# Spectral mixing with the complex filter product finished on VectorE and GpSimd, a return transform in 32-row tiles, and one fp32 copy of the filter

## The chip, the cores and the metric

The kernel runs on one core of one Trainium2 chip. A core has a matrix engine (TensorE, "PE" in the profile; its weight loads are listed apart as "PEld"), a vector engine (VectorE, "DVE"), an activation engine (ScalarE, "ACT"), a general engine (GpSimd, "POOL") and a queue engine that only starts transfers (SyncE, "SP"). Each works through its own instruction list in order. The metric is device microseconds (us) of one execution; lower is better.

## What is computed

```python
def _attn_ref(x, filt_r, filt_i):          # x: (8, 3072, 256), filters: (1537, 256)
    X = np.fft.rfft(x, axis=1)
    F = (filt_r + 1j * filt_i)[None, :, :]
    Y = X * F
    y = np.fft.irfft(Y, n=x.shape[1], axis=1)
    return y.astype(np.float32)

def _moe_ref(x, w1, w2, w_out):            # x: the result above as (24576, 256)
    h1 = x @ w1                            # w1, w2: (256, 1024)
    h2 = x @ w2
    g = np.maximum(h1, h2)
    return (g @ w_out).astype(np.float32)  # w_out: (1024, 256)
```

So each of the 8 batches is filtered along its 3072 positions (a real Fourier transform, a complex product with a filter, the transform back), and every position then goes through a maxout layer.

## The kernel before

**The transform** is split as 3072 = 96 x 32. For each batch there are four stages, all on TensorE.

- Stage 1 (`f1` for batch 1, `s1` for batches 2 to 7, `s1t` for batch 0) makes 96 numbers out of each column of 96 positions. `s1` works on half-size input: GpSimd first forms sum and difference of the two halves (`fold`, two `tensor_tensor` instructions on lines 103 and 104 for each of 8 column groups, here called quads). The result goes to DRAM (`ad`) and comes back transposed (`bt`).
- Stage 2 (`s2`) makes 32 complex frequencies of each of 24 groups `u`, for two parities `s`. Its results `px` stay in PSUM.
- The filter product (`product`, line 382) multiplies each `px` on VectorE by the real and by the imaginary filter, and leaves the four real products as `pq` in bf16. They are not added or subtracted here.
- Stage 3 (`s3`) transforms back. It reads the products with the table `VP` and then with the table `VQ` and adds both in PSUM, so the additions that a complex product needs are made by the matmul. ScalarE copies the sums out (`zt`), they go to DRAM (`zd`) and come back (`zr`, by `z_read`).
- Stage 4 (`s4`) finishes the transform with one small matmul for each of 8 blocks of 384 positions.

**The layer** runs on those blocks. For block `tt`, `moe_h(tt, j)` makes the j-th eighth of the hidden layer (two matmuls of 384 columns, `ph`), which ScalarE or VectorE passes through a ReLU (the maxout is written as `w2` part plus ReLU of the difference of `w1` and `w2`; `prep_wd` forms that difference). `moe_o` makes the output (`po`): 30 matmuls of 256 columns for each block. VectorE copies `po` out (`ot`, line 488) and GpSimd starts the transfers to DRAM (line 461).

**Order.** It is written out by hand. The loop on lines 693 to 709 goes through `tt`, and within it through 8 steps `j`. A batch so has 64 steps, numbered 8i+j. In each step come `moe_h`, then what is entered in `mid`, then three or four matmuls of `moe_o` (with the copies and output transfers that become due), then what is entered in `todo`, and at j = 4 the next `s4`. While the layer of batch b runs, `visit(b+1, n)`, entered in `mid`, makes stages 2 and 3 of the next batch in 7 visits. A visit issues `s3` of the visit before, then `s2`, then `s1` of batch b+2 for the quads that the plan names, then the products. `plan_f2` holds the steps of the visits, of the loads `load_xf`, of the folds and of the reads back. Since every engine works in order, an instruction placed in a visit holds back all that the loop issues later on the same engine. On GpSimd these are folds and output transfers; on VectorE ReLUs, output copies and the scaling of `s4`'s result (line 434).

**Array tiles.** A matmul that uses 64 rows and 64 columns of the 128 x 128 array leaves room for three others beside it. `s1`, `s2` and `s3` issue such matmuls in groups of four on different quarters.

**Buffers.** The pool `ps` has 6 PSUM banks and serves `ph`, `px`, `pa`, `pz` and `py`; `pso` has 2 for `po`. `apool` and `zpool` have 3 buffers each.

**The start.** Batch 0 goes another way: `s1t`, transposes `t1`, `s2`, the products shared by VectorE and GpSimd, `s3t`, transposes `t2`. The filter `F` is loaded by GpSimd as bf16 into half of the partitions and then doubled into the other half: two thirds of the groups by four VectorE copies, the last third by four transfers on SyncE (`double_f`, lines 130 and 132). The order on SyncE is the filter's doubling, then the layer's weights (`load_w`), then what the steps plan.

Of the kernel before, what the change touches and what calls it, by code (L numbers as in the profile page):

```python
# [13 lines left out]
B = 8  # L14
N = 3072
D = 256
# [10 lines left out]
def kernel(  # L27
# [21 lines left out]
    VP = const.tile([128, NW, 2, 64], BF16)  # L49
    VQ = const.tile([128, NW, 2, 64], BF16)  # L50
    F = const.tile([128, 2, NW, 2, D], BF16)
# [4 lines left out]
    NI = const.tile([128, 128], BF16)  # L56
    W1 = const.tile([128, 512], BF16)
    zT = const.tile([128, 2, NM, NU, 4], BF16)
    w2b = const.tile([128, 2, HID], BF16)
    w2T = const.tile([128, 8, D], BF16)  # L60
# [6 lines left out]
    pqpool = ctx.enter_context(tc.tile_pool(name="pqpool", bufs=6))  # L67
# [5 lines left out]
    pq0 = setup.enter_context(tc.tile_pool(name="pq0", bufs=6))  # L73
# [34 lines left out]
    WP = ((0, 8), (8, 12))  # L108

    def load_f(h):  # L110
        w0, w1 = WP[h]
        n = 2 * (w1 - w0)
        for g in range(2):
            for ri, f in enumerate((filt_r, filt_i)):
                k0 = 24 * g + 2 * w0
                src = bass.AP(f.tensor, f.offset + k0 * D, [[96 * D, 16], [D, n], [1, D]])
                G.dma_start(out=F[64 * g:64 * g + 16, ri, w0:w1].rearrange("p w s d -> p (w s) d"), in_=src)
                n0 = 1 if k0 == 0 else 0
                src = bass.AP(f.tensor, f.offset + (96 - k0 - n0) * D, [[96 * D, 16], [-D, n - n0], [1, D]])
                G.dma_start(out=F[64 * g + 16:64 * g + 32, ri, w0:w1].rearrange("p w s d -> p (w s) d")[:, n0:n],  # L120
                            in_=src)
                if n0:
                    src = bass.AP(f.tensor, f.offset + 48 * D, [[96 * D, 16], [1, D]])
                    G.dma_start(out=F[16:32, ri, 0, 0], in_=src)

    def double_f(h, g, ri, engine):
        w0, w1 = WP[h]
        o_, i_ = F[64 * g + 32:64 * g + 64, ri, w0:w1], F[64 * g:64 * g + 32, ri, w0:w1]
        if engine is V:
            V.tensor_copy(o_, i_)  # L130
        else:
            nc.sync.dma_start(out=o_, in_=i_)

    FN = init.tile([33, D], FP32)

    def load_fn():
        nc.sync.dma_start(out=FN[32:33], in_=filt_r[1536:1537, :])

    def fix_f():
        V.tensor_copy(F[32:33, 0, 0, 0], FN[32:33])  # L140

# [21 lines left out]
    for c in range(3, 8):  # L163
        load_x(0, c, 1)
# [575 lines left out]
```

## Time and profile before

| What | Value |
|---|---|
| Median of 3 runs | 504.04 us (503.6 to 505.15) |
| Time of the profiled execution | 503.8 us |
| Its span, first to last instruction | 502.0 us |
| TensorE busy | 488.4 us (97%) |
| VectorE busy | 331.9 us (66%) |
| ScalarE busy | 308.3 us (61%) |
| GpSimd busy | 257.5 us (51%) |
| Mean granted TensorE clock | 0.992 |
| Visit 0 of batch 1, 2, 3, 4, 5, 6, 7 starts at | 62.9, 114.6, 166.6, 224.0, 281.4, 338.8, 396.2 us |

The visits recur every 57.40 us from batch 3 on. A step without a visit takes 0.76 us when it has four matmuls of `moe_o` and 0.65 us when it has three; an `s4` adds 0.34 us. Busy time counts instructions that overlap once. A "busy" TensorE isn't at its peak, since the end of a matmul is modelled. In a timeline a row gives the start, the time to the last end, the engine, the line, the operation, what it writes and reads, its shape, the number of instructions merged and, in brackets, idle time of that engine before it with what ended it.

### The profile page before, as it was taken

The numbers are of one execution on the slowest core, as the hardware profiler recorded it, in microseconds if no ns is written. First come the engines' busy times: TensorE is split into PE (matmuls) and PEld (weight loads), VectorE is DVE, ScalarE is ACT, GpSimd is POOL, SyncE is SP. The second block draws the span as 40 slices with busy tenths as digits, with TensorE's granted clock in tenths as the row PEclk, the third lists the DMA queues.
The fourth block names the chain that finished last, engine by engine and source line by source line (L and its number), as shares of the span: only waits on it lengthen the run. The fifth ranks groups of instructions, "written<-read, shape, count | busy, mean of one in ns | idle before, by whom it ended". The sixth has DMA issues, their size and how long they took to land.

```text
span 502.0 us, 13079 instructions
## 1 busy us (share of the span) xinstructions
PE 488.4 (97%) x5299; PEld 362.1 (72%) x5303; DVE 331.9 (66%) x518; ACT 308.3 (61%) x629; POOL 257.5 (51%) x338
## 2 busy tenths in 40 slices
PE   8688999999999999999999999999999999999997
PEld 3455777777777777777777777777777777777775
DVE  7876688457865777457765687557765687555553
ACT  6776478647774676557764586647774465544442
POOL 7893569547463864645654855537632221222220
PEclk9989999999999999999999999999999999999999
DMA  7999789995799667986779558896769235411112
GB/s 125 150 252 217 230 229 290 306 274 171 212 268 260 175 204 234 250 229 189 198 244 275 187 177 245 235 239 197 197 181 255 78 111 153 168 65 64 64 64 84
DMA packets 77966, 97.20 MB, mean 194 GB/s; under 512 B 8017, under 2 KB 54354, under 8 KB 77842
## 3 DMA queue, kind: packets, MB, share of 16 engines
q1 hardware_dynamic: 64642, 66.73, 49.6%
q0 software_dynamic: 13264, 29.64, 20.3%
q8 instruction: 41, 0.67, 0.6%
q14 instruction: 19, 0.16, 0.1%
HBM read 53.87 MB, written 47.19 MB: 201 GB/s over the span
## 4 chain that ended last, share of the span: by engine, by line
PE 90%; DMA 5%; POOL 2%; issue 1%; ACT 1%; DVE 0%; SPq 0%; POOLq 0%; DVEq 0%
PE po L476 34%; PE ph L448 33%; PE po L474 8%; PE pz L399 5%; PE py L428 4%; PE pa L349 2%; DMA F<-in_filt_r_dram 2%; PE px L376 2%; DMA Wo<-in_moe_w_out_dram 2%; POOL xb L88 1%; DMA F<-F 1%; PE pr L549 1%; POOL pq L382 0%; PE pt L528 0%; PE pm__1132 L306 0%
## 5 line engine op out<-in xcount | busy, mean ns | idle before, releaser
L476 PE MATMUL po<-Wo,gt 128*128 128x256 bf16 x1536 | 261.0, 273 | 0.2 <-DMA Wo<-in_moe_w_out_dram 0.2
L452 ACT ACTIVATE gt<-ph 128x384 bf16<-128x384 f32 x321 | 157.0, 496 | 147.9 <-PE ph L448 147.3
L461 POOL DMA_DIRECT2D out_dram<-ot x186 | 102.6, 555 | 187.1 <-DVE ot L488 184.4
L476 PEld LDWEIGHTS <-gt 128*128 128x128 bf16 x1536 | 146.6, 98 | 66.1 <-issue 10.3
L450 DVE TENSOR_SCALAR gt<-ph 128x384 bf16<-128x384 f32 x191 | 104.9, 552 | 63.1 <-PE ph L448 59.9
L382 DVE TENSOR_TENSOR pq<-px,F 128x1024 bf16<-128x1024 f32 x91 | 107.0, 1219 | 24.2 <-PE px L376 22.6
L448 PEld LDWEIGHTS <-Wd 128*128 128x128 bf16 x1024 | 96.5, 98 | 12.9 <-POOL Wd L292 1.4
L103 POOL TENSOR_TENSOR xb<-XF 128x512 bf16<-128x512 f32 x48 | 61.2, 1276 | 41.3 <-DMA XF<-in_x_dram 21.2
L488 DVE COPY ot<-po 128x512 f32<-128x512 f32 x95 | 65.1, 685 | 25.3 <-PE po L476 25.0
L104 POOL TENSOR_TENSOR xb<-XF 128x512 bf16<-128x512 f32 x48 | 61.0, 1271 | 0.0
L403 ACT ACTIVATE zt<-pz 128x512 bf16<-128x512 f32 x84 | 45.6, 595 | 11.5 <-PE pz L399 8.4
L353 ACT ACTIVATE at<-pa 128x512 bf16<-128x512 f32 x96 | 51.8, 610 | 1.2 <-PE pa L349 0.8
L428 PE MATMUL py<-G,zr 96*128 96x96 bf16 x512 | 32.7, 206 | 0.2
L428 PEld LDWEIGHTS <-zr 96*128 96x128 bf16 x512 | 29.0, 97 | 2.5 <-DVE zr L552 0.4
L399 PE MATMUL pz<-pq,VP 64*64 64x256 bf16 x336 | 21.9, 281 | 0.0
L376 PE MATMUL px<-bt,U 64*64 64x256 bf16 x384 | 19.8, 278 | 1.2 <-ACT VQ L273 0.7
L399 PE MATMUL pz<-pq,VQ 64*64 64x256 bf16 x336 | 20.9, 269 | 0.0
L349 PE MATMUL pa<-xb,CT 64*64 64x512 bf16 x192 | 19.5, 383 | 0.0
L399 PEld LDWEIGHTS <-VP 64*64 64x64 bf16 x336 | 9.7, 105 | 13.3 <-issue 13.3
L376 PEld LDWEIGHTS <-U 64*64 64x64 bf16 x384 | 10.4, 109 | 3.9 <-issue 3.3
L559 PE MATMUL pd<-W 128*128 128x512 bf16 x30 | 10.5, 462 | 1.7 <-DVE zero L145 1.5
L552 DVE COPY zr<-pr 96x1024 bf16<-96x1024 bf16 (+1 forms) x8 | 5.2, 649 | 8.0 <-PE pr L549 8.0
(429 smaller groups left out, 609.7 us busy)
## 6 DMA issues: line engine op xcount, KB each, us to landing
out_dram<-ot POOLq DMA_DIRECT2D x186, 128.0 KB, 3.3
XF<-in_x_dram SPq DMA_DIRECT2D x96, 192.0 KB, 4.6
ad<-at SPq DMA_DIRECT2D x56, 192.0 KB, 3.3
bt<-ad SPq DMA_DIRECT2D x14, 768.0 KB, 9.1
zd<-zt SPq DMA_DIRECT2D x42, 256.0 KB, 2.7
zr<-zd SPq DMA_DIRECT2D x56, 192.0 KB, 4.8
WS<-in_moe_w_dram SPq DMA_DIRECT2D x4, 512.0 KB, 5.1
xb<-in_x_dram POOLq DMA_DIRECT2D x8, 192.0 KB, 5.8
```

The costliest lines, as they stand in the source:

```text
L103: G.tensor_tensor(t_[:, 0], f[:, 0], f[:, 1], OP.add)
L104: G.tensor_tensor(t_[:, 1], f[:, 0], f[:, 1], OP.subtract)
L353: S.activation(at[:, m0:m0 + 2], pa[g], AF.Copy)
L382: E.tensor_tensor(pq, px.rearrange("p (o i) d -> p o i d", o=1).to_broadcast([128, 2, 2, D]), F[:, :, 2 * v:2 * v + 2, s], OP.mult)
L399: TE.matmul(pz[g][64 * s:64 * s + 64, i], tab[64 * g:64 * g + 64, 2 * v + i, s], pq[s][64 * g:64 * g + 64, q, i], start=(q == 0), stop=(q ...
L428: TE.matmul(py[:, m], zr[b][:, 4 * i + m, 128 * dc:128 * dc + 128], G1, start=True, stop=True)
L448: TE.matmul(ph, Wd[:, dc, 128 * j:128 * j + 128], y_[:, dc], start=(dc == 0), stop=(dc == 1))
L450: V.tensor_scalar(gt[tt][:, j], ph, 0.0, None, OP.max)
L452: S.activation(gt[tt][:, j], ph, AF.Relu)
L461: E.dma_start(out=dst, in_=ot[tt // 2][:, 3 * (tt % 2) + c])
L476: TE.matmul(p_, g_[:, n - 2, blk], Wo[:, n - 2], start=(e == 0), stop=(e == 9))
L488: V.tensor_copy(ot[tt // 2][:, e - 1:e + 1], po[0])
```

## The change

What each part does:

- **Product.** `filtered` replaces `product` plus the additions in `s3`. VectorE forms the four real products of each parity in fp32 (two instructions a visit, as before), then subtracts two of them (a third instruction, bf16 result), and GpSimd adds the other two. The result `yq` is the filtered spectrum itself.
- **Tiles.** A visit now covers 4 groups `u` of which each keeps its 32 frequencies on 32 partitions. `s2` uses tiles of 64 rows x 32 columns (16 matmuls a visit where there were 8). `s3` uses tiles of 32 rows x 64 columns and is called for two visits at once, in visits 2, 4 and 6, with 4 PSUM banks. One table `VT` replaces `VP` and `VQ`.
- **Order.** `s1` comes two quads at a time, in visits 0, 1, 3 and 5. `z_read` comes in three parts. Steps of visits change; those of loads and folds stay.
- **Filter.** `F` is fp32, one row per frequency, loaded half by SyncE and half by GpSimd. Both wait for the sixth part of `x[0]`, by a copy on GpSimd into a cell that the first filter transfer overwrites. The doubling is gone; the layer's weights follow the filter on SyncE.
- **Start of batch 0.** `s3t` uses 32-row tiles with four table forms (the fourth, `VN`, is a negated one); `put_z` copies its result out.
- **Buffers.** `apool` and `zpool` go from 3 to 2. `f1_read` splits its transfer by partition halves where it split it by groups `u`.

```diff
-    F = const.tile([128, 2, NW, 2, D], BF16)
+    VT = const.tile([128, 6, 2, 2, 64], BF16)
+    F = const.tile([128, 2, 6, 2, D], FP32)
+    FN = const.tile([1, D], FP32)
...
-    pqpool = ctx.enter_context(tc.tile_pool(name="pqpool", bufs=6))
+    tpool = ctx.enter_context(tc.tile_pool(name="tpool", bufs=2))
+    wpool = ctx.enter_context(tc.tile_pool(name="wpool", bufs=4))
...
+    def load_f(q, ri, E):
+        f = (filt_r, filt_i)[ri]
+        for j in range(4):
+            k0 = 12 * j + 6 * q
+            o_ = F[32 * j:32 * j + 32, ri].rearrange("p n s d -> p (n s) d")[:, 6 * q:6 * q + 6]
+            E.dma_start(out=o_[0:16], in_=bass.AP(f.tensor, f.offset + k0 * D, [[96 * D, 16], [1, 6 * D]]))
+            n0 = 1 if k0 == 0 else 0
+            E.dma_start(out=o_[16:32, n0:6], in_=bass.AP(f.tensor, f.offset + (96 - k0 - n0) * D,
+                                                         [[96 * D, 16], [-D, 6 - n0], [1, D]]))
...
+    G.tensor_copy(F[0:1, 0, 0, 0, 0:1], xb[0, 5][0:1, 0, 0:1])
+    nc.sync.dma_start(out=FN, in_=filt_r[1536:1537, :])
     for q in range(2):
+        load_f(q, 0, nc.sync)
+        load_f(q, 1, G)
...
     def f1_read(b):
         bt[b] = bpool.tile([128, NU, D], BF16, tag="bt", name="bt")
-        for h in range(2):
-            src = ad[b].rearrange("(u q) m d -> (q m) u d", q=4)[:, 12 * h:12 * h + 12]
-            nc.sync.dma_start(out=bt[b][:, 12 * h:12 * h + 12], in_=src)
+        for s in range(2):
+            src = ad[b].rearrange("(u s r) m d -> s (r m) u d", s=2, r=2)[s]
+            nc.sync.dma_start(out=bt[b][64 * s:64 * s + 64], in_=src)
...
+    def s2(b, n):
         px = [ps.tile([128, 2, D], FP32, tag="ps", name="px%d" % s) for s in range(2)]
+        for c in range(2):
+            for j in range(4):
+                for s in range(2):
+                    u = 4 * n + j
+                    TE.matmul(px[s][32 * j:32 * j + 32, c], U[64 * s:64 * s + 64, u, 32 * c:32 * c + 32],
+                              bt[b][64 * s:64 * s + 64, u], start=True, stop=True, tile_position=(64 * s, 32 * j))
+        return px
+
+    def product(E, o_, n, s, src):
+        E.tensor_tensor(o_, src.rearrange("p (o c) d -> p o c d", o=1).to_broadcast([128, 2, 2, D]),
+                        F[:, :, n, s].rearrange("p r (o d) -> p r o d", o=1).to_broadcast([128, 2, 2, D]), OP.mult)
+
+    def nyquist(o_, px):
+        V.tensor_tensor(o_[0:1, 0, 1], px[0][0:1, 1], FN, OP.mult)
+
+    def filtered(b, n, px):
+        t_ = tpool.tile([128, 2, 2, 2, D], FP32, tag="T", name="T")
+        for s in range(2):
+            product(V, t_[:, s], n, s, px[s])
+            if n == 0 and s == 0:
+                nyquist(t_[:, 0], px)
+        y_ = wpool.tile([128, 2, 2, D], BF16, tag="yq", name="yq")
+        V.tensor_tensor(y_[:, 0], t_[:, :, 0, 0], t_[:, :, 1, 1], OP.subtract)
+        G.tensor_tensor(y_[:, 1], t_[:, :, 0, 1], t_[:, :, 1, 0], OP.add)
+        yq[b, n] = y_
+
+    def s3(b, t):
...
+        pz = [ps.tile([128, 2, D], FP32, tag="ps", name="pz%d" % j) for j in range(4)]
+        ys = [yq.pop((b, 2 * t + i)) for i in range(2)]
         for i in range(2):
+            for c in range(2):
+                for s in range(2):
+                    for j in range(4):
+                        q = (s + j) % 2
+                        TE.matmul(pz[j][64 * q:64 * q + 64, i], VT[32 * j:32 * j + 32, 2 * t + i, q, c],
+                                  ys[i][32 * j:32 * j + 32, c, q], start=(c == 0), stop=(c == 1),
+                                  tile_position=(32 * j, 64 * q))
+        zt = zpool.tile([128, 2, 4, D], BF16, tag="zt", name="zt")
+        for j in range(4):
+            S.activation(zt[:, :, j], pz[j], AF.Copy)
+        nc.sync.dma_start(out=zd[b][8 * t:8 * t + 8].rearrange("u p d -> p u d"),
+                          in_=zt.rearrange("p i j d -> p (i j) d"))
+
+    QUADS = {0: (0, 1), 1: (2, 3), 3: (4, 5), 5: (6, 7)}
+
+    def visit(b, n):
+        if n in (2, 4, 6):
+            s3(b, n // 2 - 1)
         if n < 6:
             px = s2(b, n)
         if b + 1 < B:
+            for c in QUADS.get(n, ()):
                 s1(b + 1, c)
         if n < 6:
+            filtered(b, n, px)
...
+    def s3t(n, i, pz):
+        tabs = ((0, 0, VT[:, n, :, 0]), (0, 1, VT[:, n, :, 1]), (1, 0, VT[:, n, :, 1]), (1, 1, VN[:, n]))
...
-    apool = ctx.enter_context(tc.tile_pool(name="apool", bufs=3))
-    zpool = ctx.enter_context(tc.tile_pool(name="zpool", bufs=3))
+    apool = ctx.enter_context(tc.tile_pool(name="apool", bufs=2))
+    zpool = ctx.enter_context(tc.tile_pool(name="zpool", bufs=2))
...
-    plan_f2(0, (24, 28, 31, 35, 38, 42, 46), ((0,), (1,), (2,), (3,), (4,), (5,), (6, 7)),
-            (6, 10, 14, 18, 21, 25, 29, 33), (14, 18, 21, 25, 28, 32, 36, 40))
-    for b in range(1, B - 1):
-        plan_f2(b, (7, 14, 18, 24, 31, 38, 42) if b > 1 else (14, 18, 24, 30, 34, 39, 42), ((0, 1), (2,), (3,), (4,), (5,), (6,), (7,)),
-                range(-32, 32, 8) if b > 1 else range(-25, 31, 7), range(-22, 42, 8) if b > 1 else range(-15, 41, 7))
+    plan_f2(0, (24, 28, 33, 36, 40, 43, 48), (6, 10, 14, 18, 21, 25, 29, 33), (14, 18, 21, 25, 28, 32, 36, 40))
+    plan_f2(1, (14, 19, 25, 30, 35, 39, 45), range(-25, 31, 7), range(-15, 41, 7))
+    for b in range(2, B - 1):
+        plan_f2(b, (7, 14, 20, 26, 32, 38, 44), range(-32, 32, 8), range(-22, 42, 8))
```

In `plan_f2` the first tuple holds the steps of the 7 visits, the last two ranges those of `load_xf` and `fold` for quads 0 to 7. `z_read` follows a visit with `s3` after 3 steps.

## The prediction

> **What bounds the kernel now.** I read the page's busy times and its chain first.
>
> ```profile
> PE 488.4 (97%) x5299; PEld 362.1 (72%) x5303; DVE 331.9 (66%) x518; ACT 308.3 (61%) x629; POOL 257.5 (51%) x338
> ...
> PE 90%; DMA 5%; POOL 2%; issue 1%; ACT 1%; DVE 0%; SPq 0%; POOLq 0%; DVEq 0%
> ```
>
> TensorE is the bound, and nearly without holes: whatever makes it wait is added to the span, and an engine at 66% costs nothing until one of its results is late. So two questions decide: what a visit costs TensorE, and whether each visit's inputs are there. For the first I read the timeline of TensorE over visits 0 and 1 of a batch:
>
> ```profile
> 281.42 0.41 PE L376 MATMUL px<-bt,U 64*64 64x256 bf16 x8
> 281.66 0.81 PE L349 MATMUL pa<-xb,CT 64*64 64x512 bf16 x8
> 282.40 0.50 PE L476 MATMUL po<-Wo,gt 128*128 128x256 bf16 x3
> ...
> 287.96 0.30 PE L399 MATMUL pz<-pq,VP 64*64 64x256 bf16 x4
> ...
> 288.43 0.39 PE L376 MATMUL px<-bt,U 64*64 64x256 bf16 x8
> 288.64 0.45 PE L349 MATMUL pa<-xb,CT 64*64 64x512 bf16 x4
> 289.02 0.61 PE L476 MATMUL po<-Wo,gt 128*128 128x256 bf16 x4
> ```
>
> The reader sees what each stage takes by start to next start: `s3` 0.46 us, `s2` 0.21 to 0.24, a visit with `s3`, `s2` and one quad 1.06, visit 0 (two quads) 0.98. A group of four tile matmuls of 256 columns takes 0.107 us (0.43 for four groups), the time of one full-array matmul (four `po` take 0.44). Between the last quad and `po` lie 0.38 us for 0.21 of streaming, and from the last `ph` to the first `pz` 0.255 for 0.16: a change of tile shape costs 0.096 us.
>
> For the second question, VectorE and GpSimd around visit 4 of the same kind of batch:
>
> ```profile
> 247.18 0.30 PE L399 MATMUL pz<-pq,VP 64*64 64x256 bf16 x4
> ...
> 248.07 2.36 DVE L382 TENSOR_TENSOR pq<-px,F 128x1024 bf16<-128x1024 f32 x2 [0.99 <-PE px L376]
> ...
> 250.80 0.68 DVE L488 COPY ot<-po 128x512 f32<-128x512 f32 x1
> ...
> 251.78 1.09 POOL L461 DMA_DIRECT2D out_dram<-ot  x2 [3.78 <-DVE ot L488]
> ...
> 252.88 1.28 POOL L103 TENSOR_TENSOR xb<-XF 128x512 bf16<-128x512 f32 x1
> ...
> 254.11 1.27 POOL L104 TENSOR_TENSOR xb<-XF 128x512 bf16<-128x512 f32 x1
> ```
>
> This is a chain that TensorE doesn't feel yet: products, then the output copy behind them on VectorE, then two output transfers on GpSimd, then the fold of quad 7 (step 34), done at 255.38. Visit 5 (step 38) starts at 253.73, but quad 7 is used in visit 6, at 258.29. The slack is 2.9 us.
>
> **Matmuls of a visit.** `s3` is to halve: 32 matmuls for two visits in 4 waves of eight, 0.46 us for two visits instead of 0.92. `s2` doubles its matmuls (16) and runs eight at a time: still two waves, 0.21. The trace has no 32x64 tile. Bounds: eight at once as assumed, or only four at once (`s3` as before, `s2` 0.43: +9.0 for 42 visits, and 9.7 lost in `s3`). I take eight: 64x32 tiles stand in the start (`table_v`, lines 261 and 263), where 32 matmuls of 64 columns start within 0.13 us from 19.99 on, about 4 ns apart, less than the 13.4 that `s2` needs. Three shapes now meet in visits that had one, a shape change more in each of visits 0 to 5. Visits 0, 1, 3, 5: the last `pa` bank waits anyway until the ReLU of the `ph` before the visit frees it (0.65 us after the start: the fifth bank use at 282.07), so they cost what visit 0 costs, 0.98. Visits 2 and 4: `s3`, a change, `px` waiting for the same ReLU until about 0.68, two waves and the change back, 0.99. Visit 6: 0.56 (was 0.78). A batch's visits take 4 x 0.98 + 2 x 0.99 + 0.56 = 6.46 instead of 0.98 + 5 x 1.06 + 0.78 = 7.06: **-0.6**. For batch 7, without quads, 0.34 + 5 x 0.78 + 0.56 = 4.8 becomes 4 x 0.34 + 2 x 0.99 + 0.56 = 3.9. Over batches 1 to 7: 6 x 0.6 + 0.9 = **-4.5 us**. Bounds: -7 (no cost at changes between tile shapes) to +14 (four at once).
>
> [...]
>
> **VectorE and GpSimd.** Products stay two of 1.22 us: 1024 elements from PSUM, whatever the output type (line 382 with bf16; fp32 output is not in the trace; bounds 1.22 and 1.36, twice the 0.68 of 512 elements on line 388). New is the subtraction of 512 fp32 elements from SBUF: 768 such elements take 958 ns (line 239), 192 take 351 (line 228), so 0.69. New on GpSimd is an addition of 512: a fold's row, 1.27. Totals rise by 42 x 0.69 = 29 and 42 x 1.27 = 53 us; neither engine becomes the bound over a batch (38.3 + 4.1 and about 33 + 7.6 of 57.4). What counts is what they hold back.
>
> *Quad 7.* Visit 5 now asks for quads 6 and 7 at step 38, while the fold stays at step 34. From the start of visit 4 (now step 32): `px` complete and products from 1.12 (0.89 before), subtraction done at 4.16, ReLU and copy to 5.35, transfers from 5.65 to 6.75, fold to 9.25 (2.50 a pair). TensorE reaches quad 7 after 0.99 + 0.44, four steps of 0.76 and one of 0.65, an `s4` of 0.34, `ph`, `s2` and quad 6: 6.4. It waits 2.85 us. That holds for layer batches 2 to 5, whose visits make quads for two batches on: **+11.4**. In batch 1 the fold is issued a visit earlier and I get no wait. Bounds: 4 x 2.0 (subtraction free) to 4 x 4.1 (held up by one fold of 1.27).
>
> *Scaling for `s4`.* Visit 2 lies at step 20 (j = 4), just before `s4`, whose second half VectorE scales (0.56) behind products and subtraction: done at 4.7 after the visit's start, needed by the next block's first `ph` at 4.1. Five batches x 0.6: **+3** (0 to 9).
>
> *Batch 0.* GpSimd has little room there:
>
> ```profile
> 67.88 1.26 POOL L103 TENSOR_TENSOR xb<-XF 128x512 bf16<-128x512 f32 x1 [4.49 <-PE px L376]
> 69.11 1.26 POOL L104 TENSOR_TENSOR xb<-XF 128x512 bf16<-128x512 f32 x1
> 70.32 1.11 POOL L461 DMA_DIRECT2D out_dram<-ot  x2
> 71.45 1.28 POOL L103 TENSOR_TENSOR xb<-XF 128x512 bf16<-128x512 f32 x1
> ```
>
> These are the folds of quads 2 and 3. The name in brackets can't be meant (the fold reads no `px`); the load of `XF` landed then. Until now quad 3 is used at 75.67; with the change visit 1 (step 28, at 67.6) uses it. In between GpSimd now has also the addition of visit 0: 67.88 + 2.45 + 1.1 + 1.27 + 2.45 = 75.1. So TensorE stands 7.5 us late after visit 1. Visit 0 itself waits, within that, for `bt`: the two reads of line 338 land after 5.8 and 8.4 us, at 62.65 and 65.66, and the new split needs both where visit 0 used the first alone. Following the same queue on: folds 4 and 5 end at 82.6, just before visit 3 wants them; `s4` at step 36 waits about 1.1 for VectorE; then two additions, two pairs of transfers and folds 6 and 7 end at 96.5, where visit 5 wants quad 7 at 93.2: 3.3. Less the visits' 0.6, of which half falls after visit 1, I take **+11.4** (4 to 16). The low end is a load of `XF` that lands earlier.
>
> **The start.** Gone are four VectorE copies of 1.22 (18.15 to 23.3) and the doubling transfers that held SyncE until 26.9, with the weights behind them. Added are 17 filter transfers on SyncE and 17 on GpSimd, after the sixth part of `x[0]` (11.7): by 0.5 us an issue and 5 us to land the first half is there at 21, the second at 26.5. VectorE then has 8 products and a small one, done at 32.5; before, 33.5. About 1 us is gained, and the weights come 5 us earlier, so `Wo`, whose landing at 46.6 ends a wait, comes perhaps 3 earlier. Against it stands `apool` with 2 buffers: the third `f1` buffer is written at 44.25, and the first one's last transfer, issued at 40.17, lands within at most 8.9 (line 332). ScalarE may wait up to 4.8 there. I count the start at 0 (-4 to +5), the more as the loads set when visit 1 can end.
>
> `zd` in three writes and `z_read` after step 44 cost nothing: about 11.3 us after visit 6 the first part is back (ScalarE 2.8, writing 4, reading 4.8), and `s4` comes at 14.9. Batch 0 has 2 us less; +0.5.
>
> **The sum**: -4.5 + 11.4 + 3 + 11.4 + 0 + 0.5 = +21.8. The span of 502.0 becomes 523.8; with the 1.8 us around it, 525.6, and the profiled execution (503.8) stands 0.2 under the median. I forecast **525 us**.
>
> **Rivals.**
> 1. *The folds come in time* (a GpSimd queue less backed up than I drew it, loads landing earlier). Then the matmuls decide: 504 - 4.5, with up to 3 from the start, 496 to 502; middle 499. For it: GpSimd is idle half of the time. Against it: the order in the lists, which puts a copy and two transfers ahead of fold 7. Chance 0.16. It decides if fold 7 ends under 6.4 us after visit 4 and fold 3 before 68.
> 2. *One of the two late chains only*: without batch 0's, 514; without quad 7's, 514. The middle is 513. Chance 0.20.
> 3. *Tiles don't run eight at once*: 9.0 + 9.7 on top of the forecast, 544. Against it the 4 ns. Chance 0.05.
> 4. *VectorE and GpSimd block each other.* The subtraction and the addition or a fold run at the same time, each reading two fp32 operands; no row has this pair. If one waits for the other (1.27 at most) at quad 7 (4 times), `s4` (5) and twice in batch 0, up to 14 more: 532 by half of that. Chance 0.09. [...]
>
> The forecast itself has 0.50, with a range of its own of 515 to 533.
>
> **Numbers.** 0.3%, about what this kernel's runs can tell from no change, is 1.5 us. Faster is rival 1 but for its upper edge and a tail of rival 2: 0.16. Within: 0.03. Slower: 0.81. The range 501 to 536 leaves out most of rival 1 and rival 3.
>
> **What would show it.** Right: TensorE idle before `pa` in visit 5, released by GpSimd's fold, some 2.9 us in four batches; a gap in visit 1 of batch 1's transform near 70 us; `s3` of 32 matmuls in 0.46 us; batches 3 to 5 some 2.9 us longer than 57.4. Wrong: batches shorter than 57.4 us, `pa` without idle time, or `px` groups 0.4 us long. The forecast falls as a whole if fold 7 ends before TensorE asks for it.

## The result and the profile after

The changed kernel takes **560.1 us** (median of 4 runs, 555.65 to 561.62), the kernel before 504.35 (4 runs, 503.6 to 505.15): a ratio of **1.109, 95% interval 1.102 to 1.116**. The direction was forecast, the size was not: 525 us with a range up to 536. The profiled execution took 558.84 us with a span of 557.1, so the account below is of 557.1 - 502.0 = 55.1 us.

The page of the changed kernel, busy times and the chain by engine:

```profile
PE 508.2 (91%) x5830; PEld 359.0 (64%) x5831; DVE 365.8 (66%) x564; ACT 307.3 (55%) x630; POOL 321.5 (58%) x375
...
PE 71%; DVE 9%; POOL 8%; DMA 7%; issue 3%; ACT 2%; SPq 0%; POOLq 0%; DVEq 0%; ACTq 0%
```

TensorE fell from 97% busy to 91%, and its share of the chain from 90% to 71%. VectorE (9%) and GpSimd (8%), which held 0% and 2%, are now on the path, though neither is over 66% busy: they aren't full, they are late.

Where the time came in is read from the starts of visit 0 (before in brackets, from the front table): 79.6 (62.9), 148.2 (114.6), 203.1 (166.6), 265.7 (224.0), 327.8 (281.4), 388.7 (338.8), 450.7 (396.2) us. Differences of these give the price of each stretch:

| Stretch | Before | After | Added | Forecast |
|---|---|---|---|---|
| Start, to visit 0 of batch 1 | 62.9 | 79.6 | +16.7 | 0 |
| Layer batch 0 | 51.7 | 68.6 | +16.9 | +11.4 |
| Layer batch 1 | 52.0 | 54.9 | +2.9 | 0 |
| Layer batches 2 to 5 | 57.4 each | 62.6, 62.1, 60.9, 62.1 | +18.1 | +11.4 |
| Rest | 105.8 | 106.4 | +0.6 | -1 |

(The last column sorts the forecast's terms into stretches.) What TensorE mostly waits for in the changed kernel, line and releaser, then us in total, times, and the longest:

```profile
PE pa L329 <- POOL xb L101: 9.9, 6, 2.4
PE pt L522 <- DVE T L363: 8.8, 3, 5.2
PE pa L329 <- POOL xb L102: 5.1, 6, 0.8
PE px L357 <- DMA bt<-ad: 5.0, 2, 3.6
```

The first and third row are the folds (six waits: two in layer batch 0, four later), the fourth the read back for batch 1, as forecast (1.5 us of it come before the first matmul of visit 0, so they count to the start). Layer batch 1, for which nothing was forecast, has two smaller causes: the subtraction of its fifth visit takes 2.28 us where it takes 0.69 alone, and TensorE waits 1.0 us for the scaling behind it on VectorE and 0.5 us for ReLUs. The second is the start: the return transform waits for products, and those wait for the filter, as VectorE's timeline shows:

```profile
27.70 1.22 DVE L363 TENSOR_TENSOR T<-px,F 128x1024 bf16<-128x1024 f32 x1 [8.41 <-DMA F<-in_filt_i_dram]
...
36.97 2.35 DVE L363 TENSOR_TENSOR T<-px,F 128x1024 bf16<-128x1024 f32 x2 [5.34 <-DMA F<-in_filt_i_dram]
```

The first product starts at 27.7 us (23.8 before), and the fourth stands again until 36.97. The filter's first half had landed at 27.4, its last part landed at 36.9. Busy times by stretch show what that does. A row gives the stretch and its length, then busy us (and instructions) of TensorE, its weight loads, VectorE, ScalarE and GpSimd; the last three columns are TensorE's granted clock (1.00 is full speed), the share of the 16 DMA engines and GB/s. Before:

```profile
16.00:27.00 11.00, 7.22 (x234) 5.17 (x234) 9.97 (x11) 9.10 (x17) 10.83 (x12) 0.81 0.89 139
27.00:37.00 10.00, 8.62 (x216) 5.47 (x213) 7.23 (x9) 7.53 (x15) 9.68 (x7) 0.87 0.92 272
37.00:48.00 11.00, 9.24 (x76) 5.82 (x75) 7.99 (x16) 7.54 (x14) 4.81 (x7) 1.00 1.07 212
```

After:

```profile
16.00:27.00 11.00, 4.88 (x203) 3.89 (x199) 2.93 (x5) 6.41 (x15) 4.30 (x9) 0.81 1.07 148
27.00:37.00 10.00, 4.40 (x148) 2.52 (x149) 3.93 (x5) 2.56 (x5) 8.07 (x5) 0.50 1.06 195
37.00:48.00 11.00, 6.07 (x252) 4.03 (x255) 5.81 (x5) 3.28 (x8) 10.14 (x10) 0.50 1.09 251
```

From 16 to 27 us the DMA engines are full (1.07) and move only 148 GB/s. VectorE works 2.93 us there where it worked 9.97 (4.9 of these were the doubling copies, which are gone), TensorE 4.88 where it worked 7.22, and TensorE's clock drops to half from 27 to 48.

Visit 5 of a later batch, on TensorE:

```profile
296.14 0.41 PE L357 MATMUL px<-bt,U 64*32 64x256 bf16 x16
296.49 0.41 PE L329 MATMUL pa<-xb,CT 64*64 64x512 bf16 x4
298.33 0.37 PE L329 MATMUL pa<-xb,CT 64*64 64x512 bf16 x1 [1.44 <-POOL xb L101]
299.55 0.64 PE L329 MATMUL pa<-xb,CT 64*64 64x512 bf16 x3 [0.84 <-POOL xb L102]
300.12 1.04 PE L470 MATMUL po<-Wo,gt 128*128 128x256 bf16 x4
300.95 0.85 PE L442 MATMUL ph<-y__5036,Wd 128*128 128x384 bf16 x2
```

GpSimd in the same stretch:

```profile
295.87 1.12 POOL L455 DMA_DIRECT2D out_dram<-ot  x2 [0.23 <-DVE ot L482]
297.00 1.28 POOL L101 TENSOR_TENSOR xb<-XF 128x512 bf16<-128x512 f32 x1
298.23 1.27 POOL L102 TENSOR_TENSOR xb<-XF 128x512 bf16<-128x512 f32 x1
```

This is the forecast stall: quad 6 at 296.49, then quad 7 stands for the fold that GpSimd began only at 297.0, behind two output transfers. But two `ph` then take 0.85 us where they take 0.49, since the clock is down (third column from the end, in the stretch from 300 to 302):

```profile
300.00:302.00 2.00, 2.00 (x11) 1.20 (x9) 0.06 (x1) 1.25 (x3) 1.18 (x1) 0.50 0.00 0
```

### The profile page after: what moved, and what is told of

The parts are those of the page before. It is cut to its first block, busy times and chain, and to the rows that moved or that the text cites. A ratio compares the mean times of both kernels' runs of the same rounds, so it can differ in the third digit from the quotient of the medians.

```text
span 557.1 us, 14257 instructions
## 1 busy us (share of the span) xinstructions
PE 508.2 (91%) x5830; PEld 359.0 (64%) x5831; DVE 365.8 (66%) x564; ACT 307.3 (55%) x630; POOL 321.5 (58%) x375
## 3 DMA queue, kind: packets, MB, share of 16 engines
q0 software_dynamic: 11984, 29.64, 17.9%
## 4 chain that ended last, share of the span: by engine, by line
PE 71%; DVE 9%; POOL 8%; DMA 7%; issue 3%; ACT 2%; SPq 0%; POOLq 0%; DVEq 0%; ACTq 0%
PE po L470 26%; PE ph L442 26%; PE po L468 6%; DVE T L363 5%; DMA F<-in_filt_i_dram 3%; PE py L422 3%; PE pa L329 2%; POOL yq L379 2%; PE px L357 2%; PE pz L392 2%; DMA bt<-ad 2%; POOL xb L101 2%; POOL xb L102 2%; DVE yq L378 2%; POOL out_dram L455 1%
## 5 line engine op out<-in xcount | busy, mean ns | idle before, releaser
L470 PE MATMUL po<-Wo,gt 128*128 128x256 bf16 x1536 | 265.2, 276 | 0.0
L470 PEld LDWEIGHTS <-gt 128*128 128x128 bf16 x1536 | 148.5, 99 | 67.6 <-issue 11.4
L363 DVE TENSOR_TENSOR T<-px,F 128x1024 f32<-128x1024 f32 (+1 forms) x89 | 105.1, 1215 | 40.2 <-PE px L357 26.4
L379 POOL TENSOR_TENSOR yq<-T 128x512 bf16<-128x512 f32 x42 | 68.2, 1624 | 38.4 <-DVE T L363 37.7
L378 DVE TENSOR_TENSOR yq<-T 128x512 bf16<-128x512 f32 x42 | 38.0, 904 | 1.4
L329 PE MATMUL pa<-xb,CT 64*64 64x512 bf16 x192 | 23.1, 413 | 16.5 <-POOL xb L101 9.9
L357 PE MATMUL px<-bt,U 64*32 64x256 bf16 x768 | 22.5, 282 | 7.1 <-DMA bt<-ad 5.0
L329 PEld LDWEIGHTS <-CT 64*64 64x64 bf16 x192 | 6.9, 105 | 29.7 <-issue 15.7
L357 PEld LDWEIGHTS <-U 64*32 64x32 bf16 x768 | 8.3, 89 | 20.0 <-issue 13.4
L536 ACT ACTIVATE zT<-pt 128x512 bf16<-128x512 f32 (+1 forms) x14 | 6.1, 511 | 19.1 <-PE pt L522 19.1
L522 PE MATMUL pt<-VT,T 32*128 32x64 bf16 x192 | 5.2, 235 | 10.9 <-DVE T L363 8.8
```

Source lines behind the costliest of these rows:

```text
L363: E.tensor_tensor(o_, src.rearrange("p (o c) d -> p o c d", o=1).to_broadcast([128, 2, 2, D]), F[:, :, n, s].rearrange("p r (o d) -> p r o ...
L379: G.tensor_tensor(y_[:, 1], t_[:, :, 0, 1], t_[:, :, 1, 0], OP.add)
L470: TE.matmul(p_, g_[:, n - 2, blk], Wo[:, n - 2], start=(e == 0), stop=(e == 9))
```

## The experiments

The times are single executions unless a median is given; the kernel before took 504.97, 505.22 and 504.67 us (this one a median of 7) beside them. The four executions of the changed kernel lie 6.0 us apart, so a smaller difference of two totals shows nothing by itself; what follows goes by landings, starts and the lengths of single batches. "Start" is the start of visit 0 of batch 1.

### The start: what makes the filter late

**Wide transfers.**

```diff
-        for j in range(4):
...
+        o_ = F[:, ri].rearrange("p n s d -> p (n s) d")[:, 6 * q:6 * q + 6]
+        E.dma_start(out=o_, in_=bass.AP(f.tensor, f.offset + 768 * q * D, [[6 * D, 128], [1, 6 * D]]))
```

> Here the fp32 filter is loaded by four transfers of 768 KB, each over all 128 partitions with 6 KB in one piece per partition, in place of 34 transfers over 16 partitions; the rows then come in another order, so the output is another one, with the same work. Theory (the shape of the transfers makes the filter late): the last filter part, which landed at 36.9 us in the changed kernel, lands at 25 or earlier, TensorE's clock stays above 0.8 between 16 and 48 us, visit 0 of batch 1 starts near 68 in place of 79.6, and the time is 546 to 550. Rival (its 3.1 MB are what takes the time, whatever their shape): it lands at 34 to 37, visit 0 stays at 77 to 80 and the time at 555 to 562.

Measured: **553.24 us**; the last part landed at 24.9, visit 0 started at 69.4 (-10.1). In the same stretch as above the same full DMA engines moved 399 GB/s, the layer's weights among it:

```profile
16.00:27.00 11.00, 7.13 (x269) 5.38 (x267) 8.38 (x12) 7.81 (x17) 4.99 (x3) 0.94 1.02 399
27.00:37.00 10.00, 7.34 (x305) 4.80 (x306) 5.21 (x5) 4.72 (x10) 7.66 (x6) 0.50 0.50 112
```

So the shape sets the landing. The DMA records of both traces tell that it isn't the number of transfers (4 in place of 34): a piece of 6 KB keeps a DMA engine busy for 0.23 us here (median, 16 to 27 us) and for 0.63 to 0.66 in the changed kernel. Two points missed: the clock was still 0.50 from 27 to 37, and the total fell by less than the start, because layer batches 4 and 5 took 65.4 and 63.6 us in this run.

**bf16 filter, 18 transfers of 16 partitions.**

```diff
-    F = const.tile([128, 2, 6, 2, D], FP32)
+    F = const.tile([128, 2, 6, 2, D], BF16)
-    for q in range(2):
-        load_f(q, 0, nc.sync)
-        load_f(q, 1, G)
+    for ri in range(2):
+        load_f(ri, G)
```

> The filter is held in bf16 as in the kernel before, in the changed kernel's layout: 18 transfers of 16 partitions on GpSimd, half the bytes written, no wait for the sixth part of x. If the bytes written decide, the last part lands at 24 to 27 us, visit 0 of batch 1 starts at 66 to 70 and the time is 546 to 551. If the bytes read decide (they are the same 3.1 MB), it lands at 33 to 37 and the time stays at 555 to 562. If the narrow shape decides, 18 transfers in place of 34 land at about half the time: near 25 as in the first case, which the first run has to tell apart.

Measured: **557.84 us**, last part at 29.0, start at 73.6. The landing lies between the two ranges. Half the bytes written came 7.9 us earlier, but the first transfer was also issued 4.7 us earlier (7.4 us in place of 12.1), and 149 GB/s moved from 16 to 27 us, as in the changed kernel. Without the wait for the sixth part of `x`, the three last parts of `x[0]` landed at 16.0 to 17.9 us (11.8 to 14.3 in the changed kernel). So this run doesn't tell bytes from shape.

**Forward rows only** (16 partitions as in the change, but pieces of 5 or 6 KB everywhere).

```diff
-    [[96 * D, 16], [-D, 6 - n0], [1, D]]
+    [[96 * D, 16], [1, (6 - n0) * D]]
```

> The filter is loaded as in the changed kernel, 34 transfers over 16 partitions, but the 16 transfers that read rows backwards (pieces of 1 KB) read them forwards (pieces of 5 or 6 KB); the rows of those partitions then stand in another order and the output is another one, with the same work. If the small pieces made the transfers slow, the last part lands at 22 to 27 us in place of 36.9, as with four wide transfers (24.9), and visit 0 of batch 1 starts near 69. If the 16 partitions make them slow, it lands at 33 to 37 and visit 0 stays at 77 to 80.

Measured: **561.76 us**, last part at 37.5, start at 78.9. The size of the pieces is not it; the 16 partitions are: pieces of 6 KB still take 0.65 to 0.73 us each (median, 16 to 27 us). The 96 KB transfers, issue to landing (us, median):

```profile
F<-in_filt_i_dram POOLq DMA_DIRECT2D x15, 96.0 KB, 10.0
F<-in_filt_r_dram SPq DMA_DIRECT2D x15, 96.0 KB, 9.6
```

The filter as a whole shows the same: its 3.15 MB, from 12.1 to 36.9 us, are 127 GB/s in the changed kernel, and from 13.3 to 24.9 us 271 GB/s with the wide transfers.

### The later batches: where a fold may stand

**All loads and folds four steps earlier.**

```diff
-        plan_f2(b, (7, 14, 20, 26, 32, 38, 44), range(-32, 32, 8), range(-22, 42, 8))
+        plan_f2(b, (7, 14, 20, 26, 32, 38, 44), range(-36, 28, 8), range(-26, 38, 8))
```

> The loads and folds of layer batches 2 to 6 four steps (3 us) earlier, nothing else. Theory (quad 7 waits for a fold that stands behind the visit's products, copies and transfers): the wait before quad 7, 2.6 us a batch, goes, and with it the half clock after it (1.3); the distance of the visits from 265.7 to 327.8, 62.1 us, becomes 58 to 59, and the time falls by 8 to 15 from 560 to 545 to 552. Rival (VectorE and GpSimd hold each other up wherever the fold stands): the distance stays within 1 us of 62 and the time at 556 to 562.

Measured: **576.39 us**, slower by 16. Quad 7's wait was gone as the theory said (visit 5 to the next visit 0 fell from 30.2 to 31.8 us to 27.6), but visits 0 to 2 lost more (17.3 to 19.8 us where they took 12.8 to 13.0), and layer batch 1, into which the first of the moved folds fall, took 65.3 in place of 54.9. VectorE in a visit 0:

```profile
281.15 1.20 DVE L363 TENSOR_TENSOR T<-px,F 128x1024 f32<-128x1024 f32 x1
282.39 4.02 DVE L378 TENSOR_TENSOR yq<-T 128x512 bf16<-128x512 f32 x1
286.33 0.68 DVE L482 COPY ot<-po 128x512 f32<-128x512 f32 x1
```

GpSimd beside it:

```profile
282.14 1.27 POOL L101 TENSOR_TENSOR xb<-XF 128x512 bf16<-128x512 f32 x1
283.37 1.27 POOL L102 TENSOR_TENSOR xb<-XF 128x512 bf16<-128x512 f32 x1
284.59 1.26 POOL L379 TENSOR_TENSOR yq<-T 128x512 bf16<-128x512 f32 x1
```

And TensorE after it:

```profile
287.06 0.38 PE L468 MATMUL po<-M,y__4510 128*128 128x256 bf16 x2 [1.97 <-DVE ot L482]
```

The subtraction (L378), 0.69 us alone, takes 4.02: it ends at 286.41, 0.56 us after the last of three GpSimd instructions in a row. The output copy behind it is late, and TensorE stands 1.97 us for a `po` bank. This is the mechanism of the forecast's fourth rival, beyond the size that it allowed (1.27 us at most).

**The same, with the subtraction on GpSimd.**

```diff
-        V.tensor_tensor(y_[:, 0], t_[:, :, 0, 0], t_[:, :, 1, 1], OP.subtract)
+        G.tensor_tensor(y_[:, 0], t_[:, :, 0, 0], t_[:, :, 1, 1], OP.subtract)
```

> The run with earlier loads and folds (576.4 us) showed VectorE's subtraction held for 4.0 to 5.0 us at visit 0 in each batch, until GpSimd's run of two folds and the addition was over. Here the same earlier loads and folds, and the subtraction on GpSimd, so that VectorE has no instruction with two operands in SBUF in the visits. If that hold is what made that run slow: the waits of TensorE for the output copy on VectorE (10.8 us in all) go, a batch takes 57.5 to 60 us in place of 62.7 to 65, and the time is 545 to 556. If the late loads of x are: a batch stays at 62 to 65 and the time at 570 to 580.

Measured: **549.64 us**; layer batches 2 to 5 took 58.5 to 59.1, and no wait for the output copy is left. The hold was what made the run before slow. GpSimd's addition, with a median of 1.70 us in the changed kernel, is back at 1.27.

**The subtraction as a copy of its first operand** (the second is left out of the result).

```diff
+        V.tensor_copy(y_[:, 0], t_[:, :, 0, 0])
```

> The subtraction on VectorE is replaced by a copy of its first operand (512 fp32 elements from SBUF to bf16), so VectorE reads one operand there; the second product's part is left out of the result. Theory (two operands in SBUF exclude GpSimd): the instruction takes the same time every time, 0.7 us or less, where the subtraction took 0.69 to 5.62, GpSimd's addition takes 1.25 to 1.30 where its median was 1.70, the 5.6 us hold in batch 0 goes, and the time is 550 to 557. Rival (they share bandwidth, whatever the operands): both durations still vary with what runs beside them, and the time stays within 2 us of 560.

Measured: **557.68 us**. The first expectation failed in part, as the two rows for `yq` show (shortest, median and longest in ns):

```profile
L378 DVE CAST yq<-T x42: 426/427/5278, 87.0 to 481.3; 128x512 bf16<-128x512 f32 x42
L379 POOL TENSOR_TENSOR yq<-T x42: 1254/1437/1513, 90.0 to 481.5; 128x512 bf16<-128x512 f32 x42
```

A cast with one operand is held just as long (5.28 us, the same place in layer batch 0) and still delays the addition (a median of 1.44, where it is 1.27 with the subtraction on GpSimd). My choice of a copy as a free instruction was wrong. So this run doesn't give the price of the hold: it shortens the instruction by 0.27 us, and its time lies within the scatter of the changed kernel (555.65 to 561.62).

**Only folds 6 and 7 earlier.**

```diff
-        plan_f2(b, (7, 14, 20, 26, 32, 38, 44), range(-32, 32, 8), range(-22, 42, 8))
+        plan_f2(b, (7, 14, 20, 26, 32, 38, 44), range(-32, 32, 8), (-22, -14, -6, 2, 10, 18, 25, 30))
```

> In layer batches 2 to 6 only the folds of quads 6 and 7 come earlier (steps 25 and 30 in place of 26 and 34, so each stands ahead of an addition on GpSimd in place of behind it); loads and other folds stay. Theory (the wait before quad 7 is the fold's place in GpSimd's order, and the half clock follows from that wait): the 2.6 us wait and the 1.3 us of half clock go in four batches, a batch of 62.1 us takes 58 to 59, and the time is 543 to 549. If a fold ahead of the addition holds VectorE's subtraction in its place, a batch stays at 61 to 64 and the time at 556 to 565.

Measured: **549.48 us**; layer batches 3 to 5 took 58.8, 58.1, 58.4 (batch 2 60.0). All that TensorE waits for in layer batch 4:

```profile
PE ph L442 <- ACT zt L397: 0.2, 1, 0.2
```

The fold's place in the order is the cause of the wait, and without the wait there is no half clock after it (1.00 granted in every stretch of 2 us from 325 to 383). The total came out at the edge, 0.5 us over; layer batch 1 took 57.9 us in place of 54.9, as it did (58.0) with the filter's forward rows, where nothing in that batch was changed either.

### Layer batch 0

**One quad a visit for batch 1, read back by groups.** (Quads spread as in the kernel before in all batches.)

```diff
-            src = ad[b].rearrange("(u s r) m d -> s (r m) u d", s=2, r=2)[s]
+            src = ad[b].rearrange("(u q) m d -> (q m) u d", q=4)[:, 12 * h:12 * h + 12]
-    QUADS = {0: (0, 1), 1: (2, 3), 3: (4, 5), 5: (6, 7)}
+    def quads(b, n):
+        return (((0,), (1,), (2,), (3,), (4,), (5,), (6, 7)) if b == 1 else
+                ((0, 1), (2,), (3,), (4,), (5,), (6,), (7,)))[n]
```

> Two parts of the change are undone: the quads are again spread as in the kernel before (one a visit, two in the first, and in the last for batch 1), and the read back of batch 1's first stage is again split by groups u. Theory (quad 3 in batch 0 and quad 7 later are asked for too early, and visit 0 needs the whole read back): the second wait for the read back (3.75 us), the fold waits in batch 0 (6.5) and most of its clock loss (5) go, so batch 0 takes 55 to 62 us in place of 68.6; the later batches lose their wait for quad 7 and take 58 to 59 in place of 62.1; the time is 528 to 540. Rival (GpSimd's addition and VectorE's subtraction make the visits late wherever the quads are): batch 0 stays over 65, later batches over 61, the time over 550.

Measured: **545.77 us**. Layer batch 0 fell to 60.6 (from 68.6), batches 4 and 5 to 59.5, batches 2 and 3 took 61.8 and 60.8: the theory for batch 0 held, and half of what was hoped for later, so the total missed its range. What is left in batch 0 is one wait for GpSimd's addition (3.0) and a hold of the subtraction (3.35 us in place of 0.69).

**Both engines' ends in batch 0.** Two runs on the combined kernel below move work off one of the two engines: the subtraction to GpSimd, or, for batch 1's visits, the addition to VectorE.

```diff
-        G.tensor_tensor(y_[:, 1], t_[:, :, 0, 1], t_[:, :, 1, 0], OP.add)
+        (V if b == 1 else G).tensor_tensor(y_[:, 1], t_[:, :, 0, 1], t_[:, :, 1, 0], OP.add)
```

> The combined kernel with the subtraction on GpSimd too. If the hold of VectorE is what is left of batch 0's loss (3.35 us at visit 1 in the run with one quad a visit, and 3.2 in batch 1), batch 0 and the next take 2 to 6 us less than in the combined kernel; GpSimd has 12 more instructions of 1.27 us per batch pair, which in batch 0 stand ahead of the folds. If GpSimd's queue is what is left, batch 0 takes 1 to 4 us more than in the combined kernel. Later batches: 58 to 60.

> The combined kernel (533.25 us, batch 0 62.6) with the addition on VectorE for the visits of batch 1, which lie in layer batch 0; later visits keep it on GpSimd. Theory (in batch 0 GpSimd's queue of folds, output transfers and additions is full, and the additions push the folds back): with six instructions of 1.27 to 1.7 us less there, batch 0 takes 56 to 60 us and the time is 526 to 531. Rival (VectorE, held by the folds, makes the visits late): batch 0 stays at 61 to 65 and the time at 532 to 537.

Measured: **542.56 us** with layer batch 0 at 65.6, and **541.15 us** with 66.7, against 533.25 and 62.6. Both lose. With the subtraction on GpSimd, TensorE waits 8.2 us there for GpSimd's two results (4.4 in the combined kernel); with the addition on VectorE, one addition is held for 6.05 us, and TensorE's longest waits are 6.3 and 2.7 us for the scaling on VectorE. So neither engine has room for the other's instruction in that batch. That its eight folds are what is too much was not tried.

### The parts together

**Combined:** quads one a visit for batch 1 only, read back by groups, folds 6 and 7 early (as above), and filter transfers in an order that alternates between partitions.

```diff
-        for j in range(4):
+        for h in (ri, 1 - ri):
+            for j in range(4):
...
+                p0 = 32 * j + 16 * h
...
+                E.dma_start(out=o_[p0:p0 + 16, n0:6], in_=src)
```

> The mended places together: quads one a visit for batch 1 only, the read back split by groups u, folds 6 and 7 early in the later batches, and the filter's 34 transfers, still over 16 partitions each, in another order: one queue begins with the forward rows and the other with the backward ones, and neighbours in a queue go to other groups of 32 partitions. If transfers that hit the same partitions one after another are what is slow, the filter lands at 25 to 31 us and visit 0 of batch 1 starts at 68 to 75; if any transfer over 16 partitions is slow, it lands at 34 to 37 and visit 0 starts at 77 to 80. The batches: 60 to 62 for batch 0, 55 to 57, then 58 to 59.5 each. In all 526 to 534 in the first case, 534 to 542 in the second. If the mended places only shift their waits to one another, the time stays over 545.

Measured: **533.25 us**. Last part of the filter at 34.9 and start at 74.8: the order of the narrow transfers gave 2 us of landing, so they stay slow wherever their neighbours go. Even that is not sure: in the five runs with this order the last part landed at 32.0 to 37.0 us, in the six with the changed kernel's at 36.9 to 38.4. Three of the five (this one and the two above) have the same program up to visit 0 and started it at 73.6 to 77.4, so a difference of starts below 4 us shows nothing by itself. Layer batches: 62.6, 54.8, 58.6, then 58.1 three times.

**With wide transfers** (the combined kernel with the first experiment's load; rows in another order).

> The combined kernel with the filter loaded by four transfers over 128 partitions (rows in another order, so another output, the same work). Theory (the parts add up): visit 0 of batch 1 at 69 to 70, batches as in the combined kernel, the time 525 to 531. Rival (what comes after the start depends on when it ends): visit 0 at 69 to 70 but batch 0 over 65, the time over 535.

Measured: **533.19 us**, start at 68.0, but layer batches 1 and 4 took 58.7 and 61.7 in place of 54.8 and 58.1. The 6.8 us gained at the start were lost again, and the parts don't add up: the rival was right in kind, though in other batches than it named (layer batch 0 took 60.3). The traces show what was lost: the subtraction that opens layer batch 1 is held. VectorE and GpSimd in the combined kernel:

```profile
140.76 0.97 DVE L381 TENSOR_TENSOR yq<-T 128x512 bf16<-128x512 f32 x1
141.79 1.28 POOL L101 TENSOR_TENSOR xb<-XF 128x512 bf16<-128x512 f32 x1
```

And with the wide transfers:

```profile
131.74 3.21 DVE L370 TENSOR_TENSOR yq<-T 128x512 bf16<-128x512 f32 x1
131.90 1.28 POOL L101 TENSOR_TENSOR xb<-XF 128x512 bf16<-128x512 f32 x1
```

The fold starts 1.03 us after the subtraction in the first and 0.16 us after it in the second. In layer batch 4 the second and third subtraction took 3.03 and 2.26 us where both took 0.69. In both batches the folds ahead of these wait for a load of `XF`, and they start 0.9 us earlier (layer batch 1) and 1.3 us later (4) against the visit than in the combined kernel: a shift of about 1 us goes with a subtraction of 2 to 3 us.

**TensorE kept busy at the start** (the combined kernel with more dummy matmuls ahead of each return transform).

```diff
-        TE.matmul(pz[0][:, i].rearrange("p s r c m -> p (s r c m)"), W1[:, 0:128], W1[:, 0:256], start=True, stop=True)
+        for _ in range((24, 12, 12, 12, 6, 6)[n]):
+            TE.matmul(pz[0][:, i].rearrange("p s r c m -> p (s r c m)"), W1[:, 0:128], W1[:, 0:256],
+                      start=True, stop=True)
```

> The combined kernel with dummy matmuls of 256 columns ahead of each group's return transform at the start (24, 12, 12, 12, 6 and 6 in place of one each), where TensorE waits for the products; their results are overwritten. If the half clock at the start is a loss of its own (TensorE idles, so its clock is halved, so it is slow when the products come), the clock between 26 and 48 us stays over 0.8 and visit 0 of batch 1 starts 3 to 7 us earlier than in the combined kernel without them. If the products alone set the pace there, it starts within 1 us of it, or up to 3 us later.

Measured: **539.2 us**, start at 80.7. The clock stayed up (0.81 and 0.74, third column from the end, where the combined kernel has 0.50 twice), but the start came 5.9 us later, outside both ranges:

```profile
26.00:37.00 11.00, 6.45 (x170) 4.32 (x168) 5.42 (x6) 2.55 (x5) 9.57 (x6) 0.81 1.07 208
37.00:48.00 11.00, 8.76 (x247) 6.25 (x248) 4.32 (x4) 3.28 (x8) 8.55 (x10) 0.74 1.14 256
```

The last part of the filter landed at 35.0 as before (34.9), and the last product on VectorE ended at 44.7 us in place of 42.0. The dummies take TensorE's time themselves, so the run shows that they save nothing with the narrow filter; what the half clock alone costs there stays open.

**Second-stage matmuls ahead of the return transforms** (wide filter).

```diff
     s3t(0, 0, za)
-    s3t(1, 1, za)
     pxs[4] = s2(0, 4)
+    s3t(1, 1, za)
     products(3)
+    pxs[5] = s2(0, 5)
```

> The combined kernel with the wide filter transfers (visit 0 of batch 1 at 68.0 us), and at the start the second-stage matmuls of groups 4 and 5 issued ahead of the return transforms that wait for products. Theory (what is left of the start is TensorE's order: VectorE idles 1.55 and 2.80 us for these matmuls while they stand behind a return transform that waits for GpSimd's products): the last product on VectorE ends at 32.5 to 34 us in place of 36.0 and visit 0 starts at 64.5 to 66.5. Rival (GpSimd's products or ScalarE's copies set the end there): visit 0 within 1 us of 68.

Measured: **532.96 us**. The last product ended at 32.5 us on VectorE and 33.5 on GpSimd, no later than in the kernel before (33.6 and 33.9), and visit 0 still started at 67.3. So products are not what is left of the start. The return transform then ends 4.35 us later than before (first `pa` after it at 38.72, before 34.37), and from there to visit 0 both kernels take the same time (28.6 and 28.5 us), so the smaller `apool`, for which the prediction allowed up to 4.8 us, costs nothing there. It runs at half clock (0.50 from 26 to 38 us) and waits for ScalarE's copies (`zT`) between its groups (1.1 us in two waits); which of the two costs more was not tried.

**All mends that keep the filter's rows in place** (narrow transfers; the combined kernel with both the addition and the order edit).

> The combined kernel with the 34 narrow filter transfers, with both edits of the two runs before. Theory: visit 0 of batch 1 at 70 to 75 us (the narrow filter stays), batch 0 56 to 60, later batches 58 to 59: 522 to 530 us, 3.5 to 5 per cent over the kernel before. If only one of both edits works, 528 to 534. None of the theories has it under the kernel before, since a batch without waits takes 58.1 to 58.6 us where it took 57.4.

Measured: **545.7 us** (median of 4, 542.59 to 548.08), 1.080 of the kernel before (95% 1.075 to 1.085): the addition on VectorE costs layer batch 0 its gain (67.2, as with that edit alone). Both forecasts failed: the start came at 78.9 in place of 70 to 75, with the filter's last part at 36.4, and layer batch 1 took 58.1 where the combined kernel took 54.8. How much of the start is the order of the matmuls and how much the filter isn't separated. No version beat the kernel before; the best with the rows in place is the combined one at 533.25.

## Why the prediction was wrong

**The bound and the direction: right.** In the kernel before, TensorE had hardly any holes, and what made it wait was added to the span.

**The start is the step that failed**: "I count the start at 0", with the filter's halves at 21 and 26.5 us. They landed at 27.4 and 36.9, and the start cost 16.7 us. I had priced the 34 transfers by their issue (0.5 us each) plus a landing of 5 us, as if they ran beside each other. The trace of before had the number that speaks against this: 139 GB/s from 16 to 27 us with DMA engines 0.89 busy, mostly with transfers to 16 partitions that wrote half the bytes. By that rate 3.15 MB take 23 us (an estimate), not the 14.8 from 11.7 to 26.5. The wide transfers show the cause (24.9 us, -10.1); 4.4 of the rest is the return transform, as above, and 1.5 the wait for the read back.

**Layer batch 0, +11.4 forecast, +16.9 measured**: the waits are the ones named, and their sum was near (idle time in the rows: 3.6 us for `bt` within this stretch, 3.2 for fold 3, 2.6 for fold 7; I had 7.5 together for the first two, then 3.3, and 1.1 for the scaling, which left no wait). What was missing is the clock after each wait: 0.92 on average from 84 to 148 us, some 5 us (an estimate, 0.08 of 64).

**Quad 7, 2.85 forecast, 2.6 measured**, in the four batches named (by the starts of the matmuls; the rows show 2.2 to 2.3 of it as idle time). The half clock that follows goes with another 1.2 to 1.7 in three of them (batches of 62.1 to 62.6 us, against 60.9 where the clock stayed full). Moving two folds removes both. In this I was right in mechanism and size, and left out the clock.

**Visits, -0.6 a batch forecast, -0.06 measured.** Tiles did run eight at once: 32 matmuls of `s3` took 0.58 us with the change of shape, the 16 of `s2` started within 0.14 us, and visits 2 and 4 took 0.99 and 1.05. But visits 1 and 5 cost 1.06 and 1.22 in place of 0.98, and the seven visits of before 6.93, not 7.06. So the one gain that was forecast for the later batches hardly exists. In the combined kernel a batch without waits still takes 58.1 us where it took 57.4. The 0.6 for `s4` was 0.54, in one block of each batch, though its releaser in the rows is ScalarE's `zt` copies and not the scaling on VectorE.

**Rivals.** "Folds in time" was wrong for this order of the plan, and would not have won: with the folds in time a batch takes 58.1. "One of the two late chains only" was wrong: both were late. "Tiles not eight at once" was wrong. "VectorE and GpSimd block each other" is true (0.69 us became 5.62 in layer batch 0), and larger than I allowed. In most visits the subtraction starts before the addition and takes its 0.69 us; but a hold of 2.28 us stands ahead of layer batch 1's wait, and it decided as soon as folds stood ahead of the subtraction or close behind it (the runs with earlier folds and with wide transfers on the combined kernel).

The chance and the range were too narrow because every term was a wait that I could see in the plan. The one term set at nothing was a transfer whose rate I hadn't worked out.

## What to carry to other kernels

Price a load by its bytes at the rate that transfers of the same shape reach in the trace, not by issue plus latency; ask how many partitions one transfer covers (16 gave 127 GB/s here, 128 gave 271). When a wait on TensorE is forecast, look in the trace for what the clock does after it (0.50 from 300 to 302 us here, behind the wait for quad 7). An instruction moved earlier on GpSimd can hold one on VectorE (4.02 us in place of 0.69 with all folds moved): move two folds, not eight, and look at the instruction that stands next to them.

## What the runs showed of the hardware

- The transfers to 16 partitions were slow piece by piece while the DMA engines counted as full. From 16 to 27 us a piece of 6 KB took 0.63 to 0.66 us in the changed kernel and one of 1 KB 0.12, nearly the same for each byte; over 128 partitions a piece of 6 KB took 0.23. All that moved in that stretch was 148 and 399 GB/s, with the DMA engines at 1.07 and 1.02.
- A held VectorE instruction waited not for one GpSimd instruction but for a whole run of them that follow without a gap. In layer batch 0 of the changed kernel the subtraction took 5.62 us, VectorE:

```profile
92.61 5.62 DVE L378 TENSOR_TENSOR yq<-T 128x512 bf16<-128x512 f32 x1
```

GpSimd:

```profile
91.53 1.27 POOL L101 TENSOR_TENSOR xb<-XF 128x512 bf16<-128x512 f32 x1
92.75 1.26 POOL L102 TENSOR_TENSOR xb<-XF 128x512 bf16<-128x512 f32 x1
93.97 1.25 POOL L379 TENSOR_TENSOR yq<-T 128x512 bf16<-128x512 f32 x1
95.20 1.26 POOL L101 TENSOR_TENSOR xb<-XF 128x512 bf16<-128x512 f32 x1
96.42 1.25 POOL L102 TENSOR_TENSOR xb<-XF 128x512 bf16<-128x512 f32 x1
```

Four times one GpSimd instruction ended and the next began, and the subtraction didn't come in between; it ended 0.55 us after the last of them. It isn't so every time: the subtraction of 3.21 us shown with the wide transfers ended 0.56 us after the second of two folds, though an addition follows them without a gap. What decides that the runs don't show.
- Four waits of nearly the same length on TensorE (1.4 and 0.8 us for the two halves of the fold) were followed by half clock in three batches (a mean of 0.75 to 0.79 over the 7 to 8 us from the start of that visit) and by full clock (1.00) in the fourth. What decides here the runs don't show either.
